# Another written order for the second part of a pooled-attention and softplus-FFN kernel

## The chip, the cores and the metric

One core of one Trainium2 chip runs the whole program. The metric is the device time of one execution in microseconds. The kernel before takes 865.3 us, the median of three runs (860.43 to 867.79).

## The reference

What is computed (shapes in brackets; the inputs are float32):

```python
def _attn_ref(q, k, v):                                  # [8, 8, 576, 64] each
    k_p = k.reshape(B, H, 72, 8, D).mean(axis=3)         # keys and values pooled by 8
    v_p = v.reshape(B, H, 72, 8, D).mean(axis=3)
    scores = D ** -0.5 * np.matmul(q, k_p.transpose(0, 1, 3, 2))
    scores = scores - np.max(scores, axis=-1, keepdims=True)
    attn = np.exp(scores)
    attn = attn / (np.sum(attn, axis=-1, keepdims=True) + 1e-09)
    return np.matmul(attn, v_p)

x = attn_out.transpose(0, 2, 1, 3).reshape(4608, 512)
h = x @ w_in                                             # [512, 2048]
g = np.maximum(h, 0.0) + np.log1p(np.exp(-np.abs(h)))    # softplus
out = g @ w_out                                          # [2048, 512]
```

## The kernel before

The 4608 rows of `x` are cut into 18 chunks `c` of 256 rows, the 2048 hidden columns into 8 pairs `u` of 256. Each matrix product is made of three products of rounded parts (high by high, high by low, low by high) of 128 x 128 by 128 x 256.

The kernel has two written parts. Each part makes a list of steps (`Order`), every step with an engine, a function that issues its instructions, the steps it comes after, and the buffers (`Slot`) it uses. A list of step numbers, ORDER1 or ORDER2, then says in which order the functions are called. That order is the order of every engine's queue, of SP's DMA queue as well, and it also decides which buffer a step gets. Waits between engines are derived from the order of the calls: an instruction waits for those called before it that touch the same memory. ORDER1 covers chunks 0 to 2, ORDER2 chunks 3 to 17. ORDER2 has 1970 steps: 317 of TensorE (PE), 734 of VectorE (DVE), 640 of ScalarE (ACT) and 279 of SP.

In the second part the steps of a chunk `c` and a pair `u` are these:
- `pair1` (line 719) is a block of 24 products on PE into a bank `h`. For `u` = 0 it is two halves.
- ACT takes two softplus of it (lines 727 and 741); DVE takes their difference `gl` (line 748).
- From chunk 4 on the second matrix product is a fast scheme of seven products in place of eight. It needs `sums` (four DVE steps, lines 781 to 784), their rounding on ACT (line 795) and the difference on DVE (line 800).
- `pair2_fast` (line 871), for the pair before, is a block of 21 products on PE into four banks `m`. They go in the order m[1], m[2], m[6], m[7], m[5], m[3], m[4], three products each. m[1] and m[2] share a bank, so do m[6] and m[7], and m[5] and m[3]. m[4] has the first half of the last bank. For `u` = 0 and 7 the block is two halves, of 12 and 9 products.
- After the last pair, `finish` (lines 884 and 892) adds the seven products up in two steps, and the sums are stored.

Block (c, u) of `pair2_fast` follows `pair1` of (c, u+1) on PE. Between these blocks the list places the attention of the next chunks: DVE transposes `q` (line 482), ACT copies it across in eight steps (line 493), PE makes the scores (`pair_scores`, line 515), DVE takes the least of each row (`pair_least`, line 537) and subtracts it into `E` (`pair_less`, line 553), ACT takes the exponential (line 317), DVE sums, scales and transposes (lines 1366, 1374 and 482), DMAs move the result through DRAM (lines 486 and 489), and PE makes `av_products` (lines 615 and 626). New keys and values are summed on DVE (line 214) and the keys transposed on PE (line 221).

The scores of a chunk are 16 heads' worth, and two banks hold 14 of them. The last two heads go to a third place. For chunks 6 to 17 that is the second half of the bank of m[4] of the chunk two before, `ms[old]["rest"]`. DVE's two reads of it are `pair_least` and `pair_less` with j = 2. In this text they are called the first and the second read. A POOL step (line 523) stands between the two heads' products.

`load_wi` (line 899) fetches w_in for a pair; it comes after `pair1` two pairs earlier.

Of the kernel before, what the change touches and what calls it, by code (L numbers as in the profile page):

```python
# [69 lines left out]
def pooled_attention_softplus_ffn(  # L70
# [1585 lines left out]
    for c in range(N1, NCH + 1):  # L1656
# [30 lines left out]
        0, 1, 5, 45, 14, 15, 16, 2, 3, 4, 49, 68, 23, 6, 17, 19, 321, 25, 20, 323, 18, 27, 28, 46, 47, 33, 32,  # L1687
        31, 50, 59, 48, 60, 61, 182, 318, 8, 320, 21, 101, 30, 29, 26, 69, 184, 70, 64, 65, 34, 37, 71, 41, 7,
        62, 40, 44, 42, 120, 124, 143, 38, 35, 36, 43, 39, 63, 190, 188, 187, 189, 191, 121, 122, 72, 192,
        123, 51, 52, 53, 55, 73, 74, 56, 54, 144, 145, 185, 186, 66, 365, 324, 10, 12, 327, 215, 180, 76, 75,  # L1690
        146, 77, 88, 147, 148, 152, 91, 149, 150, 89, 329, 90, 151, 268, 193, 82, 78, 84, 80, 335, 86, 57,
        153, 157, 158, 111, 94, 93, 92, 200, 112, 113, 202, 95, 114, 196, 197, 203, 201, 194, 154, 116, 155,
        102, 199, 103, 156, 198, 117, 104, 115, 96, 159, 97, 107, 99, 160, 105, 163, 204, 118, 256, 134, 98,
        100, 108, 135, 161, 136, 106, 109, 162, 165, 166, 173, 167, 168, 217, 170, 169, 125, 195, 171, 172,
        137, 139, 174, 140, 175, 126, 138, 206, 213, 214, 219, 207, 208, 210, 211, 127, 212, 209, 367, 292,
        141, 258, 176, 280, 270, 506, 220, 223, 375, 224, 221, 326, 222, 225, 337, 255, 260, 330, 267, 272,
        226, 130, 261, 262, 128, 372, 131, 227, 264, 228, 265, 373, 273, 371, 368, 274, 263, 266, 282, 132,
        294, 229, 230, 276, 231, 277, 374, 275, 242, 243, 369, 278, 234, 236, 238, 232, 279, 244, 284, 291,
        331, 285, 286, 370, 245, 287, 246, 249, 288, 376, 306, 296, 289, 248, 508, 511, 297, 247, 298, 379,
        383, 290, 382, 303, 308, 385, 377, 378, 384, 380, 300, 301, 386, 381, 299, 129, 304, 240, 250, 309,  # L1700
        513, 310, 251, 302, 253, 346, 332, 316, 387, 312, 313, 515, 311, 252, 254, 314, 334, 315, 348, 349,
        356, 357, 398, 339, 350, 351, 353, 352, 358, 354, 389, 359, 355, 396, 360, 437, 510, 516, 390, 393,
        514, 338, 394, 391, 395, 392, 363, 397, 400, 436, 447, 439, 401, 404, 402, 509, 405, 407, 403, 341,
        406, 342, 408, 344, 440, 441, 343, 409, 411, 443, 444, 512, 442, 445, 410, 446, 449, 456, 517, 450,
        453, 454, 451, 412, 423, 345, 455, 424, 457, 178, 647, 520, 452, 518, 519, 649, 459, 460, 461, 426,
        462, 425, 463, 464, 465, 430, 467, 417, 419, 769, 415, 413, 477, 524, 527, 526, 521, 428, 650, 429,
        466, 469, 470, 471, 476, 479, 522, 523, 771, 654, 427, 421, 487, 525, 472, 473, 474, 475, 431, 480,
        653, 481, 432, 483, 484, 434, 656, 433, 482, 816, 772, 435, 486, 489, 485, 774, 528, 490, 491, 492,
        497, 498, 530, 775, 539, 778, 578, 499, 494, 495, 500, 496, 493, 501, 655, 657, 531, 532, 651, 533,
        534, 535, 536, 537, 538, 541, 577, 780, 542, 652, 543, 545, 546, 548, 547, 544, 818, 777, 549, 580,  # L1710
        587, 658, 504, 588, 581, 584, 585, 582, 826, 820, 550, 586, 822, 786, 598, 957, 590, 608, 661, 583,
        591, 361, 551, 553, 558, 554, 823, 597, 600, 592, 560, 556, 618, 552, 659, 564, 594, 565, 593, 825,
        595, 596, 824, 567, 601, 665, 604, 602, 605, 819, 606, 662, 603, 566, 571, 607, 610, 617, 611, 614,
        620, 569, 821, 615, 570, 788, 664, 660, 667, 666, 663, 668, 568, 612, 616, 613, 562, 783, 628, 669,
        572, 621, 573, 575, 622, 959, 574, 624, 625, 576, 623, 626, 627, 630, 631, 638, 639, 680, 632, 635,
        640, 641, 636, 633, 634, 637, 642, 671, 678, 679, 682, 1126, 719, 643, 672, 673, 675, 785, 674, 676,
        677, 683, 686, 684, 687, 685, 688, 689, 729, 718, 721, 728, 731, 790, 739, 690, 691, 722, 725, 723,
        726, 727, 732, 724, 692, 735, 694, 738, 741, 781, 789, 736, 733, 737, 734, 742, 743, 782, 749, 701,
        695, 697, 699, 759, 703, 693, 705, 792, 708, 706, 745, 746, 747, 707, 710, 793, 744, 794, 709, 748,
        751, 758, 761, 752, 795, 753, 755, 796, 502, 797, 838, 1079, 712, 756, 711, 713, 714, 757, 754, 762,  # L1720
        716, 763, 715, 765, 717, 766, 764, 767, 768, 799, 800, 807, 808, 827, 801, 804, 802, 809, 805, 967,
        1082, 849, 810, 806, 840, 811, 803, 847, 963, 964, 960, 841, 842, 828, 830, 829, 832, 834, 844, 843,
        845, 961, 965, 966, 837, 836, 835, 833, 831, 846, 1084, 888, 645, 848, 851, 898, 852, 853, 962, 855,
        856, 858, 1081, 854, 857, 1128, 859, 887, 890, 897, 968, 891, 894, 895, 892, 1135, 1136, 1133, 1085,
        908, 1267, 900, 901, 1130, 860, 893, 862, 896, 861, 907, 910, 904, 863, 1132, 905, 902, 1129, 918,
        812, 866, 868, 864, 870, 928, 872, 1088, 1134, 906, 874, 903, 917, 920, 938, 975, 976, 971, 875, 911,
        876, 974, 1131, 877, 914, 879, 912, 913, 915, 916, 1269, 878, 921, 881, 924, 925, 880, 978, 977, 973,
        1087, 972, 922, 927, 930, 923, 969, 970, 926, 882, 931, 934, 883, 932, 935, 885, 884, 936, 933, 886,
        1090, 937, 940, 941, 948, 949, 979, 981, 1093, 1091, 942, 945, 950, 946, 943, 951, 944, 947, 952, 990,
        1096, 814, 982, 985, 983, 986, 984, 988, 987, 1095, 989, 992, 1028, 1098, 993, 1092, 994, 996, 997,  # L1730
        999, 995, 998, 1137, 1144, 1140, 1000, 1001, 1138, 1002, 1003, 1029, 1039, 1031, 1038, 1041, 1100,
        1049, 1436, 1059, 1032, 1033, 1035, 1036, 1099, 1274, 1034, 1141, 1037, 1042, 1272, 1270, 1276, 1004,
        1015, 1045, 1046, 1043, 1047, 1048, 1273, 1018, 1016, 1044, 1017, 1051, 1058, 1061, 1052, 1053, 1142,
        1055, 1021, 1056, 1022, 1020, 1019, 1062, 1102, 1057, 1143, 1139, 1054, 1007, 1009, 1011, 1005, 1069,
        1013, 1107, 1103, 1146, 1065, 1104, 1105, 1063, 1066, 1145, 1147, 1064, 1067, 1106, 1068, 1071, 1389,
        1148, 955, 1392, 1023, 1271, 1072, 1275, 1073, 1024, 1026, 1277, 1075, 1025, 1076, 1027, 1074, 1077,
        1438, 1391, 1078, 1109, 1110, 1117, 1118, 1111, 1112, 1114, 1119, 1115, 1113, 1120, 1116, 1121, 1150,
        1157, 1158, 1278, 1151, 1152, 1153, 1394, 1154, 1155, 1156, 1440, 1159, 1577, 1395, 1161, 1198, 1124,
        953, 1208, 1398, 1446, 1162, 1439, 1165, 1285, 1166, 1163, 1168, 1167, 1164, 1397, 1281, 1197, 1200,
        1207, 1210, 1169, 1279, 1218, 1403, 1201, 1202, 1442, 1204, 1205, 1170, 1203, 1206, 1171, 1445, 1444,  # L1740
        1211, 1443, 1228, 1122, 1441, 1214, 1172, 1283, 1173, 1212, 1215, 1213, 1216, 1280, 1184, 1284, 1217,
        1220, 1227, 1187, 1185, 1221, 1174, 1176, 1178, 1180, 1186, 1288, 1222, 1190, 1238, 1579, 1224, 1230,
        1182, 1223, 1191, 1225, 1226, 1400, 1282, 1231, 1237, 1248, 1232, 1406, 1234, 1287, 1235, 1189, 1188,
        1240, 1236, 1233, 1286, 1405, 1192, 1241, 1289, 1242, 1244, 1410, 1245, 1243, 1246, 1247, 1193, 1194,
        1195, 1196, 1250, 1251, 1258, 1259, 1291, 1408, 1252, 1253, 1409, 1300, 1254, 1255, 1260, 1256, 1261,
        1257, 1262, 1298, 1299, 1292, 1746, 1339, 1293, 1295, 1296, 1297, 1294, 1263, 1302, 1303, 1306, 1307,
        1412, 1338, 1265, 1349, 1304, 1305, 1308, 1341, 1309, 1310, 1348, 1359, 1342, 1343, 1345, 1311, 1346,
        1347, 1344, 1313, 1312, 1351, 1358, 1369, 1314, 1317, 1315, 1361, 1352, 1355, 1353, 1354, 1325, 1356,
        1319, 1321, 1326, 1362, 1328, 1327, 1357, 1329, 1363, 1379, 1365, 1331, 1366, 1364, 1367, 1323, 1401,
        1368, 1371, 1378, 1381, 1417, 1402, 1330, 1372, 1413, 1415, 1373, 1414, 1332, 1416, 1375, 1376, 1377,  # L1750
# [72 lines left out]
```

## Time and profile before

| | |
|---|---|
| median of three runs | 865.3 us (860.43, 865.3, 867.79) |
| profiled execution | 866.56 us, of which its span is 864.5 us |
| mean granted TensorE clock | 0.993 of full speed |
| PE busy | 844.6 us (98%) |
| DVE busy | 662.3 us (77%) |
| ACT busy | 522.9 us (60%) |
| DMA | 239 GB/s on average |

The times of the rows below are microseconds from the start of the span; a row's last brackets say how long its engine sat idle before it and what released it. "Granted clock" is the share of the full 2.4 GHz that TensorE was given. In the chain of waits, a piece is work that was on the chain that ended last, with its start and its length.

### The profile page before, as it was taken

Reading aid. Unit: us, or ns where it says so; the run is one execution under the profiler, and the core shown is the slowest. Engines: PE = TensorE matmul, PEld = TensorE weight load, DVE = VectorE, ACT = ScalarE, POOL = GpSimd, SP = SyncE. Lnnn points to the kernel's source line nnn. Section 1 sums busy time; section 2 is a strip of 40 time slices with the busy share of each in tenths; the row PEclk is TensorE's granted clock in tenths of the full one; section 3 lists DMA queues with packets and bytes.
Section 4 is the critical chain, followed back from the end, with each engine's and each line's share of the span. In section 5 each row is a group of like instructions: output and inputs, shape, how many; then the busy total and the mean of one; then the engine's idle time right before and its main releaser. Section 6 shows DMA issues by size and latency. Waiting matters only on the chain.

```text
span 864.5 us, 21237 instructions
## 1 busy us (share of the span) xinstructions
PE 844.6 (98%) x8458; PEld 820.2 (95%) x8458; DVE 662.3 (77%) x1556; ACT 522.9 (60%) x1184; POOL 3.9 (0%) x34
## 2 busy tenths in 40 slices
PE   8999999999999999999999998999898999999997
PEld 5799999999999999999999998999898999999997
DVE  6999999798987878776888776668777674766554
ACT  6943473678496577556865765466577645754532
POOL 1000000000000000000000000000000000000000
PEclk9999999999999999999999998999999999999999
DMA  9777257568998889877797897777687676566662
GB/s 273 240 221 243 75 180 244 199 200 241 333 323 271 275 283 279 258 245 260 241 291 249 266 286 236 244 258 235 209 261 226 220 242 240 197 228 246 231 232 91
DMA packets 117890, 206.90 MB, mean 239 GB/s; under 512 B 47264, under 2 KB 69280, under 8 KB 117792
## 3 DMA queue, kind: packets, MB, share of 16 engines
q1 hardware_dynamic: 117792, 205.55, 73.6%
q8 instruction: 66, 1.08, 0.5%
q14 instruction: 32, 0.26, 0.1%
HBM read 175.11 MB, written 30.41 MB: 238 GB/s over the span
## 4 chain that ended last, share of the span: by engine, by line
PE 78%; DVE 10%; ACT 6%; DMA 3%; issue 1%; SPq 0%; ACTq 0%; DVEq 0%
PE h L719 31%; PE m L871 26%; PE acc L689 7%; PE h L664 7%; PE avp L615 2%; ACT qT L493 2%; PE avp L626 1%; PE sc L515 1%; DMA kst<-in_k_dram 1%; DMA l<-wi 1%; DVE o L892 1%; PE acc L762 1%; ACT g L727 1%; DVE E L553 1%; DVE gl L748 1%
## 5 line engine op out<-in xcount | busy, mean ns | idle before, releaser
L719 PE MATMUL h<-x,l 128*128 128x256 f32 x2748 | 336.6, 279 | 0.4 <-DMA l<-wi 0.4
L719 PEld LDWEIGHTS h<-x,l 128*128 128x128 f32 x2748 | 324.7, 190 | 1.7 <-DMA l<-wi 0.6
L727 ACT ACTIVATE g<-h 128x512 f32<-128x512 f32 x120 | 71.8, 599 | 149.1 <-PE h L719 145.4
L871 PE MATMUL m<-w,so 128*128 128x256 f32 x1134 | 147.9, 277 | 0.3 <-DVE o L892 0.2
L871 PEld LDWEIGHTS m<-w,so 128*128 128x128 f32 x1134 | 137.3, 188 | 1.0 <-DVE so L800 0.5
L795 ACT CAST so<-sf 128x512 fp32r<-128x512 f32 x112 | 69.6, 621 | 74.5 <-DVE sf L784 70.8
L493 ACT COPY qT<-turn 32x256 f32<-32x256 f32 x240 | 96.9, 404 | 7.5 <-PE m L515 2.5
L800 DVE TENSOR_TENSOR so<-sf,so 128x512 fp32r<-128x512 f32 x112 | 76.9, 687 | 31.2 <-ACT so L795 30.3
L871 PE MATMUL m<-w,gh 128*128 128x256 f32 x476 | 90.5, 278 | 6.2 <-DVE E L553 6.2
L781 DVE TENSOR_TENSOR sf<-g 128x128 f32<-128x128 f32 x112 | 32.2, 287 | 74.5 <-ACT g L727 71.3
L748 DVE TENSOR_TENSOR gl<-g,gh 128x384 fp32r<-128x384 f32 (+1 forms) x120 | 67.0, 558 | 26.0 <-ACT gh L741 25.4
L871 PEld LDWEIGHTS m<-w,gh 128*128 128x128 f32 x476 | 72.0, 188 | 6.6 <-DVE E L553 6.6
L871 PE MATMUL m<-w,gl 128*128 128x256 f32 x238 | 66.2, 278 | 2.4 <-DVE gl L748 2.3
L669 ACT ACTIVATE g<-h 128x256 fp32r<-128x256 f32 (+1 forms) x96 | 32.0, 382 | 57.1 <-PE acc L689 43.9
L741 ACT ACTIVATE gh<-h 128x384 fp32r<-128x384 f32 (+1 forms) x120 | 59.5, 496 | 0.3
L664 PE MATMUL h<-x,w 128*128 128x256 f32 x396 | 49.1, 278 | 0.2 <-ACT pT L450 0.2
L664 PEld LDWEIGHTS h<-x,w 128*128 128x128 f32 x396 | 46.7, 188 | 0.9 <-ACT pT L450 0.4
L871 PEld LDWEIGHTS m<-w,gl 128*128 128x128 f32 x238 | 44.8, 188 | 2.7 <-DVE gl L748 2.7
L689 PE MATMUL acc<-w,g 128*128 128x256 f32 x264 | 46.3, 277 | 0.0
L892 DVE TENSOR_TENSOR o<-o,m 128x256 f32<-128x256 f32 x98 | 39.7, 418 | 3.3 <-ACT o L884 0.4
L689 PEld LDWEIGHTS acc<-w,g 128*128 128x128 f32 x264 | 39.8, 188 | 0.0
L871 PE MATMUL m<-l,gh 128*128 128x256 f32 x196 | 37.3, 279 | 0.0
(209 smaller groups left out, 1325.4 us busy)
## 6 DMA issues: line engine op xcount, KB each, us to landing
l<-wi SPq DMA_DIRECT2D x224, 512.0 KB
out_dram<-o SPq DMA_DIRECT2D x36, 256.0 KB
q<-in_q_dram SPq DMA_DIRECT2D x32, 256.0 KB
moved_p<-turn SPq DMA_DIRECT2D x60, 128.0 KB
pT<-moved_p SPq DMA_DIRECT2D x15, 512.0 KB
kst<-in_k_dram SPq DMA_DIRECT2D x24, 288.0 KB
vst<-in_v_dram SPq DMA_DIRECT2D x24, 256.0 KB
stage<-in_moe_w_in_dram SPq DMA_DIRECT2D x22, 256.0 KB
```

The lines of the kernel that those rows point to most:

```text
L493: nc.scalar.copy(out=o, in_=x[a * B32:(a + 1) * B32, s].rearrange("p (u m i) -> p u m i", u=T, i=B32))
L664: nc.tensor.matmul(out=ps[:, 0:CT], lhsT=row(w, kc), rhs=x[:, kc], start=first and kc == j == 0, stop=last and kc == KC - 1 and j == 2)
L689: nc.tensor.matmul(out=accs[c][t][:, ns], lhsT=a[:, ts], rhs=w[:, ns], start=f == 0 and n == j == 0, stop=f == FC - 1 and n == 1 and j == ...
L719: nc.tensor.matmul(out=ps[:, k * CT:(k + 1) * CT], lhsT=row(w, kc), rhs=x_[c][i][:, kc], start=first and n == 0, stop=last and n == len(or ...
L727: nc.scalar.activation(out=g, in_=x.rearrange("p (b i) -> p b i", i=P), func=AF.Softplus)
L741: nc.scalar.activation(out=gh, in_=quarters(c, x.rearrange("p (b i) -> p b i", i=P)), func=AF.Softplus)
L748: nc.vector.tensor_tensor(out=gl, in0=quarters(c, g), in1=gh.bitcast(F32), op=ALU.subtract)
L781: tt(out=sf[:, 2], in0=g[:, 0], in1=g[:, 2], op=ALU.add)
L795: nc.scalar.copy(out=so[:, 0], in_=ss[c, u])
L800: nc.vector.tensor_tensor(out=so[:, 1], in0=sf, in1=so[:, 0].bitcast(F32), op=ALU.subtract)
L871: nc.tensor.matmul(out=ms[c][n], lhsT=x, rhs=y, start=u == 0 and j == 0 and n in (1, 6, 5, 4), stop=u == FP - 1 and j == 2 and n in (2, 7, ...
L892: nc.vector.tensor_tensor(out=o, in0=in0, in1=m[n], op=how)
```

## The change

ORDER2 is replaced by another order of the same 1970 numbers. It is from a search in which VectorE's reads of one half of a bank and products into its other half exclude each other. Nothing else is changed: the steps, what each issues, what each comes after, and the first part are the same. The diff is 107 lines on either side; here are its beginning and the lines with the first and second reads of chunk 12 (steps 1279, 1280), chunk 14 (1589, 1590) and chunk 15 (1758, 1759).

```diff
     ORDER2 = [
-        0, 1, 5, 45, 14, 15, 16, 2, 3, 4, 49, 68, 23, 6, 17, 19, 321, 25, 20, 323, 18, 27, 28, 46, 47, 33, 32,
...
-        1207, 1210, 1169, 1279, 1218, 1403, 1201, 1202, 1442, 1204, 1205, 1170, 1203, 1206, 1171, 1445, 1444,
-        1211, 1443, 1228, 1122, 1441, 1214, 1172, 1283, 1173, 1212, 1215, 1213, 1216, 1280, 1184, 1284, 1217,
...
-        1473, 1432, 1587, 1588, 1475, 1476, 1478, 1477, 1474, 1589, 1595, 1591, 1479, 1480, 1481, 1482, 1510,
-        1528, 1716, 1511, 1512, 1514, 1513, 1515, 1590, 1516, 1517, 1520, 1527, 1530, 1483, 1593, 1594, 1494,
...
-        1894, 1892, 1652, 2028, 1669, 1758, 1620, 1621, 1622, 1623, 1655, 1896, 1653, 1656, 1895, 1890, 1762,
-        1654, 1759, 1766, 1679, 1657, 1763, 1624, 1635, 1893, 1662, 1663, 1625, 1631, 1627, 1629, 1664, 1665,
...
+        14, 15, 321, 0, 1, 2, 5, 45, 50, 16, 323, 3, 17, 6, 4, 19, 23, 46, 47, 25, 18, 20, 48, 318, 51, 59,
...
+        1190, 1286, 1188, 1231, 1189, 1191, 1232, 1234, 1283, 1289, 1233, 1235, 1241, 1192, 1236, 1446, 1279,
+        1244, 1245, 1246, 1280, 1193, 1242, 1194, 1243, 1247, 1250, 1195, 1406, 1196, 1251, 1258, 1252, 1253,
...
+        1514, 1515, 1521, 1482, 1513, 1589, 1516, 1594, 1597, 1528, 1716, 1483, 1596, 1524, 1494, 1527, 1530,
+        1497, 1525, 1598, 1707, 1711, 1495, 1522, 1538, 1490, 1531, 1488, 1484, 1486, 1523, 1526, 1496, 1590,
...
+        1896, 1676, 1638, 1724, 1678, 1689, 1637, 1766, 1677, 1681, 1758, 1633, 1640, 1682, 1683, 1727, 1684,
...
+        1735, 1736, 1759, 1779, 1733, 1770, 1777, 1771, 1772, 1741, 1778, 1781, 1895, 1891, 1774, 1773, 1775,
...
```

In these lines 1207, 1217, 1247 are the blocks `m` of chunk 10 for the pairs 2, 3 and 6; 1210 is `pair1(10,4)`, 1241 the softplus of `pair1(10,7)`; 1214, 1215, 1216 are the sums of pair 4, their rounding and its difference, 1213 is its `gl`; 1192 are the attention products of chunk 11.

## Rows read from the trace of the kernel before

**Rows 1.** The page, first part: busy us (share of the span) and instructions.
```profile
PE 844.6 (98%) x8458; PEld 820.2 (95%) x8458; DVE 662.3 (77%) x1556; ACT 522.9 (60%) x1184; POOL 3.9 (0%) x34
```
**Rows 2.** Whom PE waited for, 178 to 865 us: total, times, longest.
```profile
PE m L871 <- DVE E L553: 6.2, 2, 3.6
PE m L871 <- DVE gl L748: 2.3, 1, 2.3
PE m L515 <- ACT qT L493: 0.5, 1, 0.5
PE h L719 <- DMA l<-wi: 0.4, 1, 0.4
...
```
**Rows 3.** Stretches of 20 us: busy us by engine, granted clock, DMA share, GB/s.
```profile
520.00:540.00 20.00, 17.21 (x166) 16.91 (x166) 12.89 (x33) 9.56 (x25) 0.00 (x0) 0.83 0.72 237
...
600.00:620.00 20.00, 17.41 (x190) 17.00 (x189) 15.54 (x39) 11.58 (x23) 0.10 (x1) 0.91 0.61 211
...
660.00:680.00 20.00, 17.58 (x150) 16.99 (x149) 15.26 (x40) 15.26 (x38) 0.00 (x0) 1.00 0.71 237
```
**Rows 4.** Chain of waits, 512 to 683 us: start, length, what.
```profile
512.07 2.39 PE m L871 x21
...
523.80 4.97 PE h L719 x24
...
613.87 4.34 PE h L719 x24
...
657.91 2.39 PE m L871 x21
673.77 2.72 PE h L719 x24
...
681.59 1.02 PE avp L615 x16
682.62 0.67 PE avp L626 x4
```
**Rows 5.** Timeline, 514 to 666 us: start, length, engine, line, operation [idle before].
```profile
514.48 0.31 DVE L537 TENSOR_REDUCE mn<-m 128x2 f32<-128x144 f32 x1 [0.69 <-PE m L871]
...
522.43 0.30 DVE L553 TENSOR_TENSOR E<-m,mn 128x144 f32<-128x144 f32 x1
...
522.79 0.80 PE L871 MATMUL m<-w,gh 128*128 128x256 f32 x2 [3.58 <-DVE E L553]
...
613.25 0.50 PE L871 MATMUL m<-w,gh 128*128 128x256 f32 x2 [2.59 <-DVE E L553]
...
660.33 0.31 DVE L537 TENSOR_REDUCE mn<-m 128x2 f32<-128x144 f32 x1 [3.97 <-PE m L871]
...
665.53 0.39 PE L871 MATMUL m<-w,gl 128*128 128x256 f32 x1 [2.29 <-DVE gl L748]
```
**Rows 6.** DVE and ACT by line and shape: busy us, mean ns | idle before.
```profile
L800 DVE TENSOR_TENSOR so<-sf,so 128x512 fp32r<-128x512 f32 x112 | 76.9, 687 | 31.2 <-ACT so L795 30.3
L748 DVE TENSOR_TENSOR gl<-g,gh 128x384 fp32r<-128x384 f32 x112 | 61.5, 549 | 25.6 <-ACT gh L741 25.0 <-issue 0.2
L892 DVE TENSOR_TENSOR o<-o,m 128x256 f32<-128x256 f32 x98 | 39.7, 418 | 3.3 <-ACT o L884 0.4
L781 DVE TENSOR_TENSOR sf<-g 128x128 f32<-128x128 f32 x112 | 32.2, 287 | 74.5 <-ACT g L727 71.3 <-DMA out_dram<-o 2.4
L537 DVE TENSOR_REDUCE mn<-sc 128x7 f32<-128x504 f32 x30 | 19.9, 673 | 0.9 <-PE m L515 0.5 <-PE sc L515 0.4
L482 DVE STREAM_TRANSPOSE turn<-pm 128x1024 f32<-128x1024 f32 x15 | 18.6, 1240 | 0.7 <-ACT qT L493 0.6
...
L493 ACT COPY qT<-turn 32x256 f32<-32x256 f32 x240 | 96.9, 404 | 7.5 <-PE m L515 2.5 <-DVE turn L482 0.8 <-PE sc L515 0.6
L727 ACT ACTIVATE g<-h 128x512 f32<-128x512 f32 x120 | 71.8, 599 | 149.1 <-PE h L719 145.4 <-DVE o L892 2.8 <-ACT qT L493 0.2
L795 ACT CAST so<-sf 128x512 fp32r<-128x512 f32 x112 | 69.6, 621 | 74.5 <-DVE sf L784 70.8 <-issue 1.1 <-PE m L871 1.0
```

200 rows, old and new, of the table ORDER2 are left out of this document.

## The prediction

> **What bounds the kernel now.** The page first: TensorE is busy for 844.6 of 864.5 us [rows 1], so only what it loses, by waiting or by a lower clock, can be won by another order of the same instructions. The second part, whose order is changed, begins at about 177 us. Next I read who TensorE waits for from there on [rows 2]. Two lines hold nearly all of it: 6.2 us in two waits on the write of `E` in line 553, and 2.3 us in one wait on line 748; the others are 0.5 us or less. So DMA, ScalarE and the weight loads hold nothing up to speak of, and VectorE does so at three places only.
>
> The stretches of 20 us around these places then show the clock [rows 3]: its mean is 0.83 of full speed in one and 0.91 in another, so a part of each ran at the lower of the two levels, 1.2 GHz, and it is 1.00 in the third. The chain of waits gives what each place cost in all, against undisturbed blocks of 2.72 us (24 products into `h`) and 2.39 us (21 into `m`) [rows 4]:
> - **A**, at 512 us: a block `m` ends at 512.07 + 2.39 = 514.46, so the next `h` and `m` should end at 519.57. The `h` after them starts at 523.80, 4.23 late, and takes 4.97 where 2.72 is usual, 2.25 more. Together 6.48.
> - **B**, at 613 us: a wait of 2.59 [rows 5], and the `h` behind it takes 4.34, 1.62 more [rows 4]. Together 4.21.
> - **C**, at 660 us: after a block `m` that ends at 657.91 + 2.39 = 660.30, two pairs of 5.11 should bring the third `h` at 670.52; it starts at 673.77, 3.25 late.
>
> The sum is 13.9 us. 8.5 of it is the three long waits (3.58, 2.59, 2.29) [rows 5], 4.5 is the slower clock of A and B (6.48 - 3.58 + 1.62), and 1.0 is what small waits behind C add.
>
> **Why it waits there.** One bank holds the product `m[4]` in one half and two heads' scores (`rest`) in the other. VectorE reads the scores twice, least (line 537) and difference (line 553); the waits show that a read and a product in the other half stand in line for each other, as they come in the list. In A VectorE's first read starts at 514.48, when the block before has ended, and the second at 522.43; the last three products of the next block start at 522.79, when it is over [rows 5]. B ends on such a second read too. In C the first read itself holds VectorE up for 3.97 us, until the block before it is done; what stands behind it in the queue is late, and TensorE waits for line 748.
>
> In the old list the first and second reads of A (steps 1279 and 1280) have 11 VectorE steps between them, some fed by `pair1(10,4)`, the very block that runs just before the waiting one. From the end of that `h` only the 18 products ahead of `m[4]` cover them: 18 x 2.72 / 24 = 2.04 us. The chain is a softplus 0.60, four `sums` of at most 1.15 together, a rounding 0.62, a difference 0.69, the read 0.30 [rows 5, 6]: 3.36, and other steps stand among them. So A follows from the list.
>
> **What the change moves.** The 1970 written steps are the same ones, so no engine gets more work. TensorE's 317 stay nearly as they are: all the FFN blocks keep their order, and only five steps are moved: the scores of chunks 7 and 12 and three key transposes (by 2 to 6 blocks; the scores of 12 from behind the first block of chunk 10 to behind its third). The longest common order is 410 of VectorE's 734 steps, 392 of ScalarE's 640 and 191 of SP's 279. The change is thus a new sequence of the engines around an unchanged TensorE, whose waits of now are all the above.
>
> **The reads in the new list**, part by part. Twelve chunks (6 to 17) share the bank.
> - Chunk 12 (A now): both reads stand behind `pair1(10,7)` and the attention products of chunk 11, before block `m` (10,6). From the end of the block `m` before it, TensorE has 2.72 + 1.69 (1.02 + 0.67) [rows 4] + 2.04 = 6.45 us until it needs the second read. VectorE, through the same chain behind `pair1(10,7)`: 2.72 + 3.36 = 6.08. It fits, with 0.4 to spare.
> - Chunk 14 (B now): the second read comes a block `m` and a block `h` after the first, so no one block has to cover both. But the difference 12,4 that `m` (12,4) needs stands behind a transpose of 1.24 [rows 6] and a key sum; there I find no room to spare.
> - Chunk 15 (C now): the first read is moved from `m` (13,2) to (13,4), behind which no long row of VectorE stands; the second behind the last block of chunk 13. From there VectorE has a difference 0.69, the read 0.30, a difference 0.55 and four output sums of 0.42 [rows 6], 3.2 us, and a rest of the output sums before it; TensorE needs that bank after 2.72 + 1.36 = 4.08. It fits narrowly.
> - Chunk 10: behind the first read stand a least of 0.67, a small difference under 0.30 and the differences 0.69 and 0.55 that block (8,5) needs: with the read 2.5, against 2.72 and the products before their use. It fits by some 0.4.
> - Chunks 6, 7, 8, 9, 11, 13, 16 and 17 come out in the same way with 0.5 us or more.
>
> So the three places are to go: **-13.9 us**, the largest term. No edit of TensorE's own work stands against it.
>
> **What it adds.** Where VectorE's first read waits for a block, all VectorE steps behind it wait as well. There are seven such first reads in the new list (chunks 7, 8, 10, 12, 14, 15, 17) and five in the old (6, 8, 10, 12, 15). ScalarE: the turned copies of chunk 4 now come after the transpose that stands behind `pair_low(3,0)`; sixteen of 0.404 [rows 6] are 6.5 us, which ends about when TensorE asks for the scores of chunk 4. SP: each of the 112 loads of `wi` is issued in a queue whose last TensorE step lies at least two `m` and one `h` block, 7.5 us, ahead of its reader, in both lists; the one such wait now is 0.4 us [rows 2]. I cost the moved DMAs at nothing; their cover is these 7.5 us, and without it a late load costs what the one of 0.4 does, or a wait as in B. POOL's one step per chunk follows the scores and moves with them. For the new small waits nothing in the trace is a measure: at the low end none, at the high end one more place such as A (6.5). I take five narrow places (chunks 4, 10, 12, 14, 15), each missed by one VectorE step of 0.55 to 0.69, so **+2.9 us**, nearest to the small waits that the old list has at its narrow places.
>
> **The sum.** The profiled execution takes 866.56 us (864.5 of span and 2.06 around it): 866.56 - 13.9 + 2.9 = 855.6. That execution lies 1.26 above the median of 865.3, so on the median's footing 854.3.
>
> **The clock's share.** 4.5 of the 13.9 us are the slow clock behind A and B, while C, with a wait of 2.29, shows no drop [rows 3, 5]. The Trainium skill, TensorE: Matmul & The Clock Gate, section "What's actually happening", says that the activity watch behind the clock runs freely, so where its change falls differs from run to run. By that rule the clock's share needn't be in every run of before, and the gain would be 9.4 + 0 to 4.5, before the 2.9; that the three runs lie between 860.43 and 867.79 doesn't speak against it.
>
> **Rivals.**
> 1. One new long wait. At a narrow place VectorE comes late enough for a wait with a slow clock, at the mean price of the three, 4.6, or A's 6.5: 858.9 to 860.8, within 1%. For it: margins of 0 to 0.4 us at the places above, and that a wait of 2.59 already took the clock down. Against it: outside the bank the old list left no TensorE wait over 0.5.
> 2. The clock's part is not in a usual run of before: 865.3 - 9.4 + 2.9 = 858.8, within 1%.
> 3. Slower: the first reads hold VectorE. A held first read cost VectorE 3.97 us in C, and there are seven now. If each passes on a place of 4.6 us, the time is 851.4 + 2.9 + 4.6n; it is over 1% slower (above 873.95) from five places on, at 877.3. Against it: at those seven the steps behind the read are short, as counted.
> 4. The bank isn't what TensorE waits for and the places remain: 865. Against it stands the end of the second read 0.06 us before the products start in A.
>
> **How the numbers follow.** The forecast, 854.3, gets 0.58, rival 1 0.26, rival 2 0.09, rival 3 0.05, rival 4 0.02. The forecast's own range is 850 to 857 (no new waits, 851.4, with a little less of the small ones; or twice the narrow ones). The range reaches over rivals 1 and 2 and their narrow waits: 849.5 to 863. A measurement here can tell about 1%, 8.7 us. Faster by over 1% (under 856.6): the forecast and a little of 1 and 2, 0.60. Within 1%: 0.34. Slower: 0.06.
>
> **What would show it.** Right: no TensorE wait on line 553 over 0.5 us, a granted clock of 1.00 in all stretches after 177 us, VectorE's waits of line 537 on `m` short or harmless, and blocks of 5.11 us in a row. Wrong: TensorE waits on lines 748 or 800 (a queue behind a first read), on the copies of line 493, on `l<-wi`, or a clock under 1.00 at a new place.

## The result, and the profile after

The changed kernel takes 853.64 us, the median of four runs (851.85 to 855.0); the kernel before took 864.15 us beside it (median of four, 860.43 to 867.79). The ratio is 0.9877, with a 95% interval of 0.983 to 0.9925. The forecast was 854.3. The profiled execution takes 853.57 us, with a span of 851.6, against 866.56 and 864.5. One run of the kernel before, of 1405 us at a mean clock of 0.557, stands in no figure of this text.

The page's first lines, busy time by engine, and the first line of its chain, the shares of the span on it:

```profile
span 851.6 us, 21249 instructions
...
PE 840.1 (99%) x8458; PEld 816.3 (96%) x8458; DVE 661.4 (78%) x1556; ACT 524.1 (62%) x1184; POOL 3.9 (0%) x34
...
PE 91%; DVE 4%; DMA 2%; ACT 2%; issue 0%; SPq 0%; DVEq 0%; ACTq 0%
```

The instructions are as many as in [rows 1], and VectorE and ScalarE do the same work to within 1.2 us. TensorE is busy for 4.5 us less, as much as its slower blocks behind A and B had cost. The rest of the 12.9 us of span, 8.4, is idle time that is gone. Whom TensorE waited for from 178 us on (total, times, longest):

```profile
PE m L871 <- DVE gl L748: 0.5, 1, 0.5
PE m L515 <- ACT qT L493: 0.5, 1, 0.5
```

Of [rows 2] the 6.2 us on line 553, the 2.3 on line 748 and the 0.4 on `l<-wi` are gone. The three stretches of [rows 3] now (start and end, length, busy us of PE, PEld, DVE, ACT and POOL, granted clock, DMA share, GB/s):

```profile
520.00:540.00 20.00, 20.00 (x214) 19.70 (x213) 14.67 (x41) 13.36 (x34) 0.00 (x0) 1.00 0.94 268
600.00:620.00 20.00, 20.00 (x180) 20.00 (x179) 16.71 (x41) 13.03 (x30) 0.00 (x0) 1.00 0.86 285
660.00:680.00 20.00, 20.00 (x184) 19.36 (x183) 12.22 (x37) 11.87 (x30) 0.00 (x0) 1.00 0.61 218
```

TensorE is busy all through, at full clock; every stretch from 177 to 840 us shows 1.00 (the last, from 840 on, shows 0.94, with TensorE done at about 847). The chain at place A, which stands against [rows 4] (start, length, what):

```profile
519.37 2.72 PE h L719 x24
522.09 2.38 PE m L871 x21
524.47 2.72 PE h L719 x24
527.19 2.38 PE m L871 x21
529.57 2.72 PE h L719 x24
532.29 1.06 PE avp L615 x48
533.36 1.01 PE avp L626 x8
```

Blocks follow each other every 5.10 us. The reads of chunk 12 against those of [rows 5], from the timeline of VectorE and of TensorE:

```profile
533.02 0.30 DVE L537 TENSOR_REDUCE mn<-m 128x2 f32<-128x144 f32 x1
...
535.54 0.30 DVE L553 TENSOR_TENSOR E<-m,mn 128x144 f32<-128x144 f32 x1
...
536.40 0.40 PE L871 MATMUL m<-l,gh 128*128 128x256 f32 x2
```

The first read has no idle time before it in brackets: it waits for no block. The second ends at 535.84, and the products into that bank start at 536.40, 0.56 us later. The forecast had counted 0.4 to spare. From 178 us on the first reads on `m` wait for nothing, where VectorE had lost 7.9 us to four such waits before:

```profile
DVE mn L537 <- PE m L871: 7.9, 4, 4.0
```

### The profile page after: what moved, and what is told of

Its sections match the earlier page's. It is cut to its first block, busy times and chain, and to the rows that moved or that the text cites. A ratio compares the mean times of both kernels' runs of the same rounds, so it can differ in the third digit from the quotient of the medians.

```text
span 851.6 us, 21249 instructions
## 1 busy us (share of the span) xinstructions
PE 840.1 (99%) x8458; PEld 816.3 (96%) x8458; DVE 661.4 (78%) x1556; ACT 524.1 (62%) x1184; POOL 3.9 (0%) x34
## 4 chain that ended last, share of the span: by engine, by line
PE 91%; DVE 4%; DMA 2%; ACT 2%; issue 0%; SPq 0%; DVEq 0%; ACTq 0%
PE h L719 37%; PE m L871 31%; PE acc L689 7%; PE h L664 7%; PE avp L615 2%; PE sc L515 2%; PE acc L762 2%; PE avp L626 1%; DMA w<-t 1%; DMA stage<-in_moe_w_out_dram 1%; DMA t<-t 1%; PE m L515 0%; PE warm L309 0%; ACT qT L493 0%; DVE x L638 0%
```

## The experiments

**What was in dispute.** The theory says that the three places are what the change wins, each because a read of the bank comes too late or too early, and that the rest of the new order adds next to nothing. One rival says that the gain comes from the new sequence as a whole (some 600 moved steps). Another says that the clock's share is not in a usual run. A third says that the bank isn't what decides.

Each kernel was timed beside the kernel before on the same chip. There were two sets, on two chips: the changed kernel again, the three places together, only A and A put back in the first, where the kernel before had a median of 865.35 (16 runs), and the other four in the second, where it had 865.04 (18 runs). The ratios are worked out with their intervals and are not the quotients of these medians.

| kernel | median us | ratio (95%) | span of the profile | its mean clock |
|---|---|---|---|---|
| the changed kernel again | 852.68 | 0.9859 (0.9826 to 0.9893) | 849.4 | 1.000 |
| three places mended in the old list | 854.6 | 0.9882 (0.9843 to 0.992) | 852.0 | 1.000 |
| only A mended | 862.06 | 0.9971 (0.9947 to 0.9995) | 860.9 | 0.995 |
| only B mended | 862.69 | 0.9961 (0.9943 to 0.9978) | 861.5 | 0.993 |
| only C mended | 860.21 | 0.9939 (0.9918 to 0.9959) | 857.5 | 0.995 |
| new list with A put back | 856.19 | 0.9889 (0.9856 to 0.9922) | 853.4 | 0.999 |
| old list, m[4] first | 869.27 | 1.0055 (1.0035 to 1.0076) | 869.7 | 0.993 |
| new list, m[4] first | 858.85 | 0.9927 (0.9904 to 0.9951) | 854.3 | 1.000 |

**Three places mended in the old list.** Four numbers of the old list are moved, and everything else of it stays. 1280, 1590 are second reads, 1758 a first read; 1172 is a small VectorE step of chunk 11 that stood ahead of 1280.

```diff
 A
-    1171, 1445, 1444, 1211, 1443, 1228, 1122, 1441, 1214, 1172, 1283, 1173, 1212, 1215, 1213, 1216, 1280, 1184,
+    1171, 1172, 1280, 1445, 1444, 1211, 1443, 1228, 1122, 1441, 1214, 1283, 1173, 1212, 1215, 1213, 1216, 1184,
 B
-    1513, 1515, 1590, 1516,
+    1513, 1515, 1516,
...
-    1523, 1496,
+    1523, 1590, 1496,
 C
-    1669, 1758, 1620,
+    1669, 1620,
...
-    1618, 1651,
+    1618, 1758, 1651,
```

Expected: 

> The list of before with four numbers moved and nothing else: the second read of chunk 12 (with the product of the last keys of chunk 11 that frees its buffer) right behind the main product, ahead of the sums of pair 4; the second read of chunk 14 behind the differences of pair (12,4), past the block it held up; the first read of chunk 15 right behind the scores, past which no block stands. Theory (the three places are the whole gain): no TensorE wait on lines 553 or 748 over 0.5 us, granted clock 1.00 in all stretches after 177 us, a profiled time near 853.5, that is 866.56 less 13.9 plus about 1, and 852 to 856 in the median, the same as the new list. Rival (the 700 other moved steps of VectorE, ScalarE and SP matter as well): it stays at 858 or above.

Measured: 854.6 us, ratio 0.9882, whose interval lies over that of the new list (0.9859). TensorE's waits from 178 us on:

```profile
PE m L871 <- DVE gl L748: 1.5, 1, 1.5
PE m L515 <- ACT qT L493: 0.4, 1, 0.4
PE avp L615 <- DVE E L553: 0.3, 2, 0.2
```

No wait of TensorE for the bank is left, and profile and median (854.11 and 854.6) came as expected. Four moved numbers do what the new list does, to within what can be measured; the other moved steps add nothing that shows. One expectation, no wait over 0.5 us on line 748, was missed: I had not foreseen the wait of 1.5 us there, at 528.58. The second read of A now runs earlier, but the other VectorE steps that stood before it are still there, and the next thing late is `gl`.

**The places one by one.** The same edits, each alone.

Only A. Expected: 

> The list of before with the place A alone mended (two numbers moved, chunk 12). Theory (three places that add up): the wait of 3.6 us on line 553 and the slow clock behind it are gone, B (2.6 us and its clock) and C (2.3 us) stay; about 6.5 us less than before in the profile, 860, and ratio to before 0.992 to 0.995. Rival (one place's wait is only passed on to the next): ratio 0.998 to 1.002.

Only B. Expected: 

> The list of before with place B alone mended (one number moved: the second read of chunk 14 past the block (12,2) that waited for it, behind the differences of pair (12,4)). Theory: the wait of 2.6 us on line 553 at about 613 us and the slow clock behind it are gone; a wait of up to 1 us on line 748 or 800 may follow one block later, since VectorE's queue there is as long as before; A and C stay. 3 to 4.2 us less in the profile, ratio 0.994 to 0.998. Rival (the wait is passed on in full): a wait of 2 us or more at the next block.

Only C. Expected: 

> The list of before with place C alone mended (one number moved: the first read of chunk 15 right behind the scores, where it waits for no block). Theory: VectorE isn't held there for 4 us, TensorE's wait of 2.3 us on line 748 at about 665 us is gone, none takes its place on line 553; A and B stay as they were. About 3 us less in the profile, ratio 0.995 to 0.999. Rival (VectorE is too late there anyway): a wait of over 1 us on line 748 or 553 stays at C.

TensorE's waits with only A mended, its three stretches (columns as above), and then the chain at place C in it (start, length, what):

```profile
PE m L871 <- DVE gl L748: 3.5, 3, 2.3
PE m L871 <- DVE E L553: 2.1, 1, 2.1
```

```profile
520.00:540.00 20.00, 18.79 (x197) 18.00 (x197) 15.78 (x40) 11.69 (x30) 0.00 (x0) 1.00 0.90 300
600.00:620.00 20.00, 17.91 (x195) 17.63 (x194) 14.59 (x38) 9.58 (x17) 0.10 (x1) 0.91 0.65 213
660.00:680.00 20.00, 19.48 (x158) 18.84 (x159) 11.78 (x30) 14.00 (x36) 0.00 (x0) 0.91 0.62 208
```

```profile
660.00 0.47 DVE gl L748
660.47 0.04 issue
660.52 4.04 PE m L871 x19
```

A's wait and its slow clock are gone, and B and C stay. But a wait of 1.07 on `gl` has come behind A, as in the kernel with all three mended, and place C, at 1.00 in [rows 3], now runs at 0.91: 19 products take 4.04 us, where 21 took 2.39. So the gain was 3.6 us in the profile (866.56 to 862.92), not the 6.48 of A; 1.07 and the 1.9 that the slower products cost at C (4.04 less 19 x 0.113) are about what is missing. The expected ratio, 0.992 to 0.995, was missed by 0.002 on the small side. Its interval reaches into the rival's 0.998 to 1.002 too, so the time doesn't decide here; the rows show that of A's wait a part, 1.07 of 3.58, was passed on.

With only B mended, waits and stretches:

```profile
PE m L871 <- DVE E L553: 3.6, 1, 3.6
PE m L871 <- DVE gl L748: 2.8, 2, 2.3
...
```

```profile
520.00:540.00 20.00, 17.02 (x161) 16.89 (x165) 12.76 (x33) 9.45 (x25) 0.00 (x0) 0.83 0.71 236
600.00:620.00 20.00, 20.00 (x231) 19.80 (x230) 17.93 (x47) 12.99 (x25) 0.10 (x1) 1.00 0.78 258
660.00:680.00 20.00, 19.18 (x153) 18.33 (x154) 12.02 (x32) 13.62 (x34) 0.00 (x0) 0.91 0.61 203
```

B is gone, clock and all, and no wait of over 0.5 us follows it until C; the profile fell by 3.0 us (866.56 to 863.54) and the ratio is 0.9961, both as expected. C, which was not touched, again shows a drop. With only C mended, VectorE's waits of line 537 and TensorE's:

```profile
DVE mn L537 <- PE m L871: 3.9, 3, 2.8
```

```profile
PE m L871 <- DVE E L553: 5.7, 2, 3.6
...
PE m L871 <- DVE gl L748: 0.4, 1, 0.4
```

The held read of 3.97 and the wait on line 748 that it caused have gone together: C was the first read, as the theory has it. Its gain of 4.8 us in the medians is more than the 3.25 that C cost in the profile of before, and the expected 0.995 to 0.999 was missed on the other side. The first stretch was at 0.91 in this execution where it was at 0.83 in [rows 3], and B's wait was 2.09 us here, as with only A mended, where it was 2.59 in [rows 5]. So a part of this gain is not C's.

Taken singly the places are worth 0.29%, 0.39% and 0.61%, together 1.29%; mended at once they gave 1.18%, and the new list 1.23 and 1.41%. They add up within the intervals, but the split among them does not follow one profile, and it is not settled: by the medians alone A would be worth 0.38% and B 0.27%. In the profiles what the slow clock takes moves from place to place.

**A put back into the new list.** The first read goes behind `pair1(10,4)`, the second behind the sums and differences of that pair, and the blocks that stood between go behind the sums as well, as in the old list.

```diff
-    1446, 1279, 1244, 1245, 1246, 1280, 1193,
+    1446, 1244, 1245, 1246, 1193,
...
-    1278, 1210, 1217, 1228, 1220, 1180,
+    1278, 1210, 1279, 1228, 1180,
...
-    1172, 1213, 1281,
+    1172, 1213, 1280, 1217, 1220, 1281,
```

Expected: 

> The new list with place A put back: both reads of chunk 12 ahead of block (10,3), the second behind the sums and the difference of pair (10,4). Theory: one TensorE wait on line 553 at that block. From the end of pair1(10,4): softplus 0.60, its rounding 0.48, a copy 0.83, the rounding of the sums 0.62, differences 0.69 and 0.55, the product of the ends 0.28, the read 0.30 is 4.35 us, against 2.04 of cover, so 2.3 us of wait, and 0 to 3 us of slow clock behind it: 856 to 859, ratio to before 0.990 to 0.995. Rival (the place of the reads doesn't matter): the same as the new list, 0.988, and no such wait.

TensorE's waits, VectorE's two reads and the products that waited, from the timeline, and the 20 us behind:

```profile
PE m L871 <- DVE E L553: 2.3, 1, 2.3
PE m L515 <- ACT qT L493: 0.5, 1, 0.5
```

```profile
518.96 0.27 DVE L537 TENSOR_REDUCE mn<-m 128x2 f32<-128x144 f32 x1
...
522.12 0.30 DVE L553 TENSOR_TENSOR E<-m,mn 128x144 f32<-128x144 f32 x1
...
522.48 0.50 PE L871 MATMUL m<-w,gh 128*128 128x256 f32 x2 [2.27 <-DVE E L553]
```

```profile
520.00:540.00 20.00, 17.73 (x192) 17.23 (x192) 12.92 (x37) 13.85 (x35) 0.00 (x0) 1.00 0.79 258
```

The wait is back at its place with the expected 2.3 us, and it is the only one of its kind. The clock stayed at 1.00 in this execution, so this time it cost the wait and no more. The time rose by 3.5 us in the medians against the new list beside it, whose interval it overlaps. The ratio, 0.9889, lies just outside the expected 0.990 to 0.995 and no farther from the rival's 0.988, so it is the wait that speaks against the rival, and not the time.

**The products of m[4] first in each whole block.** This moves the use of the shared bank by 18 products and leaves every list as it is. For VectorE's second read the cover gets 2.04 us shorter; a first read is released 2 us earlier, since the block's last product no longer goes into that bank.

```diff
-        def fn(which=(1, 2, 6, 7, 5, 3, 4)):
+        def fn(which=(4, 1, 2, 6, 7, 5, 3) if 0 < u < FP - 1 else (1, 2, 6, 7, 5, 3, 4)):
```

In the old list, expected: 

> The list of before; in the blocks m of pairs 1 to 6 the three products of m[4] come first and not last. Theory (reads and the products of m[4] stand in line for each other, as the list has them): a second read is covered by 2.04 us less, and a first read is released 2.04 us sooner. So A's wait grows from 3.6 to about 5.6 and B's from 2.6 to about 4.6, both on line 553, while C (where the first read held VectorE) goes from 2.3 to 0.3 or less; VectorE's waits of line 537 on m fall from 7.9 to below 3. Time: waits 10 to 11 in place of 8.5, 2 to 5 us over before. Rival (the reads wait for a whole block, or a block for the reads, wherever m[4] stands): waits of A, B and C as before, ratio 1.0.

TensorE's three waits at the places, from the timeline, then VectorE's first reads in all and the one at C:

```profile
526.95 0.77 PE L871 MATMUL m<-w,gh 128*128 128x256 f32 x2 [5.37 <-DVE E L553]
...
617.25 0.80 PE L871 MATMUL m<-w,gh 128*128 128x256 f32 x2 [4.13 <-DVE E L553]
...
670.63 0.48 PE L871 MATMUL m<-w,gh 128*128 128x256 f32 x2 [0.78 <-DVE E L553]
```

```profile
DVE mn L537 <- PE m L871: 2.6, 2, 1.9
```

```profile
665.13 0.31 DVE L537 TENSOR_REDUCE mn<-m 128x2 f32<-128x144 f32 x1 [1.93 <-PE m L871]
```

A grew from 3.58 to 5.37 (expected 5.6) and B from 2.59 to 4.13 (expected 4.6; from the 2.09 that B had in two other kernels it is 2.04 more). At C, the place of the first read, VectorE is held for 1.93 in place of 3.97, 2.04 less, and TensorE's wait of 2.29 on line 748 is gone. In its place stands one of 0.78 (expected 0.3 or less), now on the second read of chunk 15, which this edit covers less. The two kinds of read move in opposite directions, by about the 2.04 us. A wait that had nothing to do with this bank would not; the rival that the bank doesn't decide is out. The median rose by 4.2 us (869.27 against 865.04), within the 2 to 5 expected. Not foreseen was a wait of 1.07 on ScalarE's copies at 259, where the kernel before has 0.53.

In the new list, expected: 

> The new list with the same edit: m[4] first in the blocks of pairs 1 to 6. Theory: the narrowest second read, chunk 12's (0.4 us to spare by the sum of the forecast), is now 1.6 us late; chunk 11's first read may cost a wait of under 1; the others have room. Waits on lines 553 and 537 of 1.5 to 3 us in all, none over 2.1, 855 to 857 us or 0.988 to 0.992 of before. Rival (the new list has ample room everywhere): no wait on line 553.

The two longest waits for the bank, from the timeline:

```profile
468.18 0.47 PE L871 MATMUL m<-w,gh 128*128 128x256 f32 x2 [1.66 <-DVE mn L537]
...
537.24 0.48 PE L871 MATMUL m<-l,gh 128*128 128x256 f32 x2 [1.62 <-DVE E L553]
```

Chunk 12 waits 1.62 where 1.6 was expected: 2.04 less cover, less about 0.5 that was to spare. So the margin of 0.4 to 0.56 us, counted from rows, was real. Missed: chunk 11's first read makes TensorE wait for 1.66 (expected under 1), the waits on the two lines come to 3.6 (expected 1.5 to 3), and the median of 858.85 is above the 855 to 857 expected; the profiled execution took 857.47.

**The new list again.** Expected: 

> The new list again, beside the others. Both theories: ratio to before 0.983 to 0.992, no TensorE wait over 0.6 us after 177 us, granted clock 1.00.

Measured: 852.68 us, ratio 0.9859, clock 1.00 in all stretches until TensorE is done. The expected limit on waits was missed: the wait on `gl` among the blocks of chunk 4, 0.50 in the first profile, is 0.87 in this one, at 243.04.

```profile
PE m L871 <- DVE gl L748: 0.9, 1, 0.9
```

This kernel is the one that the others of its set are compared with.

**How much of the clock's loss is in every run.** The mean granted clock of the 34 runs of the kernel before in the two sets, and their times:

| mean clock | runs | time us |
|---|---|---|
| 0.997 | 3 | 861.76 to 863.2 |
| 0.995 | 15 | median 864.56 |
| 0.994 | 1 | 867.14 |
| 0.993 | 11 | median 865.53 |
| 0.991 | 3 | 865.39 to 871.02 |
| 0.989 | 1 | 869.94 |

None reaches 0.998. Of the ten runs of the new list, nine are at 0.999 or 1.000 and one, of 855.0 us, at 0.997. So a usual run of before does lose time to the clock, but not always the same: over the whole span, with the waits and the end where TensorE is done, 0.003 x 862 = 2.6 us of full clock are missing at one end and 0.011 x 870 = 9.6 at the other, and 0.007 x 865 = 6.1 in the profiled execution. With A put back the clock was 1.000 or 0.999 in three of the six runs, and 0.997 or 0.998 in the other three. Whether its wait is what took the clock down in those three is not shown: they have no rows, and one run of the new list without this wait had 0.997 too.

## Why the prediction was right

**The three places, -13.9 us.** Right. In the profiles the second part fell from 687.5 us (864.5 less its begin at 177.0) to 674.1 (851.6 less 177.5), 13.4 less. The first part, whose list is the same, came out 0.5 longer. None of A, B and C is left, mending them alone gives the gain of the new list, and putting A back brings its wait back.

**The clock's 4.5 us in it.** Right for the two profiles, where TensorE's busy time fell by 4.5 (in part by chance: some of the small waits behind C count as busy time, and the slow pace of the last section added 1.25). As a property of the kernel it is a mean: place C kept 1.00 in the profile of before and fell to 0.91 in two kernels whose C was untouched, and A's stretch was 0.83 twice and 0.91 once. Rival 2, that a usual run has none of it, is out by the table of clocks. The Trainium skill, TensorE: Matmul & The Clock Gate, section "What's actually happening", has the watch run freely, so that the place of a change differs from run to run. The traces agree: C's wait of 2.29 left its stretch at 1.00 in the profile of before, and the same wait stood in one of 0.91 with only A and with only B mended. That the medians moved less (10.5 to 12.7 us) than the two profiles (13.0) fits with this: 19 of the 34 runs of before have a mean clock above the 0.993 of the profiled one.

**The narrow places, +2.9 us.** Too large. All TensorE's waits after 178 us come to 0.98, and neither of the two is at a place that I had named: one, 0.50, is on `gl` at 243.85, among the blocks of chunk 4 (what I had named there were the copies ahead of its scores), the other, 0.48, on ScalarE's copies at 257.86, ahead of the scores of chunk 6. One like it, 0.5, stood in [rows 2] as well. The five margins that I had counted held: 0.56 was left for chunk 12 (6.83 us of cover and 6.27 of VectorE's chain, where I had counted 6.45 and 6.08; the attention products of chunk 11 took 2.07, and I had used the 1.69 of another chunk), and shortening the cover there by 2.04 made a wait of 1.62. The step that failed was to take each narrow place as missed by one VectorE step: 2.9 us was put for waits there, and the new waits come to 0.5 (0.9 in the second profile). My counts of the longest common order were too small as well: it is 448, 418 and 192 steps and not 410, 392 and 191, but no term goes by them.

**The sum.** -13.9, with 0.5 for the new wait on `gl` and -0.4 for the load of `wi` that no longer waits, gives -13.8 for the second part. To it come 1.25 us by which more blocks ran at the slow pace of the last section (2.4 us in this trace, 1.15 in that of before), which leaves 0.9 us of the 13.4 that I can't assign. That the median came within 0.7 us of the forecast owes something to chance: the term that was too large by 2.4 and the smaller share of the clock in a usual run go against each other.

**Rival 1**, one new long wait: none. It was the nearest to come true all the same: the old list with four numbers moved got such a wait, 1.5 us on `gl`, with the clock at 1.00. **Rival 3**, held first reads: none is held in the new list; and in the kernel with three places mended, three are held for 3.9 us in sum, and its one longer wait comes 14 us after the last of them. **Rival 4**: out by the order of the seven products. **The moved DMAs, at nothing**: right; no wait on a load is left.

## What to carry to other kernels

Where TensorE is busy for 98%, go through its few long waits and ask of each which read or write in a shared bank comes late or is held, and how many products cover it, counted to the product that touches the bank and not to the end of the block; here four numbers of a list of 1970 held the gain, to within its interval. A held read costs by what stands behind it in its queue, so its price shows up as a wait on another line. A gain that contains time at the lower clock should be given a width, since it varies between executions of one kernel, and mending one place can be followed by a drop at another.

## What the hardware showed that I had not expected

At a granted clock of 1.00 some stretches run at a slower pace. The chain of the new list in its first profiled execution, and then in its second (start, length, what):

```profile
553.65 2.83 PE h L719 x24
556.48 2.47 PE m L871 x21
...
574.85 2.83 PE h L719 x24
```

```profile
552.47 2.72 PE h L719 x24
555.19 2.38 PE m L871 x21
...
572.87 2.72 PE h L719 x24
```

The same products take 118 ns each (2.83 / 24) in the first and 113 in the second. The pace changes at places that differ between executions of one kernel, and it lasts from one block to some 30 us. Over the second part it is worth 2.4 us in the first execution and 1.2 in the second, about half of the 2.2 us between their spans (851.6 and 849.4). What starts and ends it I did not find.
